# Attention's first loads in another order, its constants made later, and one load of the second layer issued 1.7 slots earlier

## Chip, cores and metric

One core of a Trainium2 chip. The metric is device time in microseconds of one launch, the median of the timed runs. Five engines run side by side: TensorE (PE in the rows, its weight loads PEld), VectorE (DVE), ScalarE (ACT), GpSimd (POOL) and SyncE (SP, which here only issues DMAs). Each runs its own instructions in order and waits on semaphores for the others.

## What is computed

```python
def _attn_ref(q, k, v, phi):           # q, k, v: (8, 8, 576, 64), phi: (8, 8, 576, 32)
    a = np.exp(phi - np.max(phi, axis=2, keepdims=True))
    a = a / (np.sum(a, axis=2, keepdims=True) + 1e-09)
    k_m = np.einsum('bhsm,bhsd->bhmd', a, k)
    v_m = np.einsum('bhsm,bhsd->bhmd', a, v)
    scores = q @ k_m.T / 8;  attn = softmax(scores)
    return attn @ v_m
...
x = attention, as (4608, 512)
x = top-1 mixture of 8 experts of x (w1, w2), times its gate      # moe_
g = elu(x @ w_in);  out = g @ w_out                               # moe2_: 512 -> 2048 -> 512
```

All of it is float32.

## The kernel before

Attention runs over 8 units (`Attn.units`: a pair of batches by half of the heads). What a unit does is cut into steps, methods of `Attn` (L1620 to L1946), and two written lists set the order in which the steps are emitted: `PROLOGUE` for unit 0 and the first pieces of unit 1, then `ORDER` once for each unit, with offsets. A step that stands in `PROLOGUE` is not emitted again by `ORDER`: `attn_items` keeps the first of equal entries. Each engine then runs its instructions in the order in which they were emitted.

The steps that matter here, for unit 0 in their order of need:

- `load_phi`, `load_kv`, `load_q` issue the unit's loads from SP: phi in 2 DMAs of 288 KB into tile `ft`, k and v in 4 of 576 KB into `kv`, q in 2 of 576 KB into `qt`. The tiles have two buffers each, so the loads of unit n+2 wait for the reader of unit n. The hardware DMAs share 8 semaphores in turn, so a DMA also waits until the eighth before it has landed.
- `soft_max` (DVE, the maximum of `ft`), `soft_max_t`, `soft_diag`, `soft_bcast` (PE and DVE, the maximum over all positions), `soft_exp` (DVE subtracts, ACT writes `e`), `soft_sum` (POOL).
- `kvm` (PE, 72 small products of `kv` and `e` into `pkvm`), `kv_sum` (PE), `kv_norm` (DVE, ACT), `kv_t` (PE transposes, ACT writes `kT`, `vT`), `v_gate` (PE with `wgd`, the gate's weights).
- `qtr` (PE transposes q, ACT copies it out as `qT`), `scores` (PE), `scores_exp` and `norm` (DVE, ACT), `attn_t` and `av` (PE, ACT).
- `warm` is products of a tile of ones, only to keep PE busy.

`setup_consts` (L52) runs ahead of all this. It loads the gate's weights `wg` (16 KB), and makes the identity, a triangle `trib`, and tables of numbers: POOL writes each as int32 (`IOTA`), DVE casts it (`iota_f`, L78). All of these but two use one scratch tile `i32`, so that each IOTA waits for the cast before it.

After attention come the experts (TensorE in float32r pieces) and the two layers of the FFN (class `Ffn`), each product by a 7-multiplication scheme, and each operand in two parts, `his` (ACT) and `los` (DVE or POOL). The second layer walks over 36 sets k (9 token tiles by 4 pieces of the hidden dimension). For set k, ACT issues two loads from DRAM tensor `g_d`: `load_g` (768 KB into `los`) and `load_a21` (256 KB into `scr`). Then ACT writes `his` of the three loaded pieces, DVE makes four sums out of `los` and `scr` (`left_sums`, L846 to L849), ACT writes `his` of those, and DVE writes `los` twice (L1271). Only then can PE run the set's 7 products (`prod_out`, L1332 to L1334 for both layers). Sets alternate between two halves of `his` and `los`. The weights `wu` of the last piece (7 DMAs of 512 KB from `woc_d`, L1220) are issued from SP during sets 1 and 2.

The order in the FFN is that of a heap of events with times in slots (a slot is one product); `out_set` puts set k's events at `base(k) = 252 + 7k + 2`, and emits the loads of set k+2 there:

```python
        if 0 < k < NU * NJ - 2:
            ev(b + 3.2, self.load_g, k + 2)
            ev(b + 3.3, lambda: self.load_a21(k + 2, self.scr[k % 2][:, 2]))
        if k and k + 1 < NU * NJ:
            ev(b, self.prep_g, k + 1, b, ev)
```

`prep_g(k+1)` has its events at b (sums), b+0.1 (`his` of the loaded pieces), b+2.0 (`his` of the sums) and later.

Of the kernel before, what the change touches and what calls it, by code (L numbers as in the profile page):

```python
# [37 lines left out]
NT36 = N // P  # L38
# [12 lines left out]

def setup_consts(ctx, tmp_ctx, tc, g, w_gate):  # L52
    nc = tc.nc
    g.cp = ctx.enter_context(tc.tile_pool(name="cp", bufs=1))
    cp = g.cp
    g.ident = cp.tile([P, P], F32, name="ident")
    make_identity(nc, g.ident)
    g.ones = cp.tile([P, P], F32, name="ones")
    nc.vector.memset(g.ones, 1.0)
    g.onesb = cp.tile([P, P], BF16, name="onesb")  # L60
    nc.vector.memset(g.onesb, 1.0)
    g.trib = cp.tile([P, P], BF16, name="trib")
    nc.gpsimd.affine_select(
        out=g.trib, in_=g.onesb, pattern=[[1, P]], compare_op=ALU.is_gt,
        fill=0.0, base=0, channel_multiplier=-1,
    )
    g.wg = cp.tile([P, H // 2, E], F32, name="wg")
    nc.sync.dma_start(g.wg, w_gate.rearrange("(hp r) e -> r hp e", r=P))
    g.wgd = cp.tile([P, H // 2, 2, E], F32, name="wgd")
    nc.gpsimd.memset(g.wgd, 0.0)  # L70
    for h in range(2):
        nc.gpsimd.tensor_copy(g.wgd[64 * h : 64 * h + 64, :, h, :], g.wg[64 * h : 64 * h + 64])
    g.sel = cp.tile([P, 64], F32, name="sel")
    nc.vector.tensor_tensor(out=g.sel, in0=g.ident[:, :64], in1=g.ident[:, 64:], op=ALU.add)
    tmp = tmp_ctx.enter_context(tc.tile_pool(name="ctmp", bufs=1))
    i32 = tmp.tile([P, 128], I32, name="i32")

    def iota_f(name, shape, pattern, base=0, cm=0, dtype=F32):  # L78
        n = 1
        for s in shape[1:]:  # L80
            n *= s
        t = cp.tile(shape, dtype, name=name)
        iv = i32[:, :n]
        nc.gpsimd.iota(iv, pattern=pattern, base=base, channel_multiplier=cm)
        flat = t
        if len(shape) == 3:
            flat = t.rearrange("p a b -> p (a b)")
        nc.vector.tensor_copy(flat, iv)
        return t

    g.rev8 = iota_f("rev8", [P, E], [[-1, E]], base=E)
    g.i128 = iota_f("i128", [P, P], [[1, P]], dtype=BF16)
    g.i36 = iota_f("i36", [P, NT36], [[1, NT36]])
    g.i36b = iota_f("i36b", [P, NT36], [[1, NT36]], dtype=BF16)
    g.kW = iota_f("kW", [P, N // W], [[W, N // W]])
    g.k96 = iota_f("k96", [P, NEARLY * T // 96], [[96, NEARLY * T // 96]], base=96)
    g.tslot = iota_f("tslot", [P, NWIDE + NXMAX], [[1, NWIDE + NXMAX]])
    nid = tmp.tile([P, NT36], I32, name="nid")
    nc.gpsimd.iota(nid, pattern=[[2 * S, B // 2], [1, 9]], base=0, channel_multiplier=9)
    nhi_i = tmp.tile([P, NT36], I32, name="nhi_i")  # L100
    nlo_i = tmp.tile([P, NT36], I32, name="nlo_i")
    nc.vector.tensor_scalar(out=nhi_i, in0=nid, scalar1=6, scalar2=None, op0=ALU.arith_shift_right)
    nc.vector.tensor_scalar(out=nlo_i, in0=nid, scalar1=63, scalar2=None, op0=ALU.bitwise_and)
    g.nhi = cp.tile([P, NT36], BF16, name="nhi")
    g.nlo = cp.tile([P, NT36], BF16, name="nlo")
    nc.vector.tensor_copy(g.nhi, nhi_i)
    nc.vector.tensor_copy(g.nlo, nlo_i)

    g.dram = ctx.enter_context(tc.tile_pool(name="dram", bufs=1, space=DRAM))
    g.x_d = g.dram.tile([N, XW], F32, name="x_d")  # L110
    g.y_d = g.dram.tile([DM, N + PAD], F32, name="y_d")
    g.ord_d = g.dram.tile([N + PAD], I32, name="ord_d")
    g.wic_d = g.dram.tile([NU, P, 7, 2, 2, CW], F32, name="wic_d")
    g.woc_d = g.dram.tile([NU, P, 7, 2, 2, CW], F32, name="woc_d")
    g.g_d = g.dram.tile([NJ, NU, P, 4, 512], F32, name="g_d")
    padz = tmp.tile([1, PAD], I32, name="padz")
    nc.vector.memset(padz, 0)
    nc.sync.dma_start(g.ord_d[N:].rearrange("(o n) -> o n", o=1), padz)
    g.oh = cp.tile([P, NT36, E], BF16, name="oh")
    g.colx = cp.tile([P, NT36], F32, name="colx")  # L120
    nc.vector.memset(g.colx, float(NEARLY * T))


def one_hot(tc, g, pool, lg, bp):
# [184 lines left out]
class Rest:  # L309
# [357 lines left out]
class Small:  # L667
# [18 lines left out]
    def gate(self):  # L686
        self.xn = self.m.x_gate(self.xg)
# [480 lines left out]
class Ffn:  # L1168
# [322 lines left out]
    def out_set(self, k, ev):  # L1491
        b = self.base(k)
        pe = [(1, 0), (2, 1), (4, 2), (6, 3), (7, 4), (5, 5), (3, 6)]
        if k == 0:
            pe = [(1, 0), (2, 0.5), (7, 4), (4, 5), (6, 6), (5, 7), (3, 10.8)]
        if k == NU * NJ - 1:
            pe = [(1, 0), (6, 1), (7, 2), (5, 3), (4, 4), (2, 5), (3, 6)]
        if k == 1:
            pe = [(1, -1), (2, 0), (4, 1.4), (6, 3), (7, 4), (5, 5), (3, 6)]
        for c, at in pe:  # L1500
            ev(b + at, self.prod_out, k, c)
        if 0 < k < NU * NJ - 2:
            ev(b + 3.2, self.load_g, k + 2)
            ev(b + 3.3, lambda: self.load_a21(k + 2, self.scr[k % 2][:, 2]))
        if k and k + 1 < NU * NJ:
            ev(b, self.prep_g, k + 1, b, ev)
        if k % NU == NU - 1:
            ev(b, self.evacuate, k // NU, b, ev)
# [124 lines left out]
class Attn:  # L1633
# [61 lines left out]
                u.qt[:, 2 * b : 2 * b + 2].rearrange("p q i d -> p q (i d)"), self.rows(self.src[0], u, b)  # L1695
            )

    def load_qkv(self, u):
        self.load_kv(u)
        self.load_q(u)  # L1700

    def new(self, u):
        u.xt = self.xbp.tile([P, 2, 9, WV], F32, tag="xt", name="xt", bufs=3)

# [23 lines left out]
    def gate(self, u):  # L1728
        self.gate_oh(u)
        self.gate_x(u)  # L1730

    def soft_max(self, u):
        mx = self.sp.tile([P, 4, M], F32, tag="mx", name="mx")
        m4 = self.sp.tile([P, 4, 4, M], F32, tag="m4", name="m4", bufs=1)
        op = self.tc.nc.vector.tensor_tensor
        ft = u.ft
        op(out=m4, in0=ft[:, :, 0:4, :], in1=ft[:, :, 4:8, :], op=ALU.max)
        op(out=m4[:, :, 0:2, :], in0=m4[:, :, 0:2, :], in1=m4[:, :, 2:4, :], op=ALU.max)
        op(out=mx, in0=m4[:, :, 0, :], in1=m4[:, :, 1, :], op=ALU.max)
        op(out=mx, in0=mx, in1=ft[:, :, 8, :], op=ALU.max)  # L1740
        u.mx = mx
# [208 lines left out]


PROLOGUE = [
    ("load_q", 0),
    ("warm", 0, 0, 15),
    ("load_phi", 0),
    ("load_kv", 0),
    ("load_phi", 1),
    ("load_q", 1),
    ("load_phi", 2),
    ("warm", 0, 1, 4),  # L1960
    ("soft_max", 0),
    ("soft_max_t", 0),
    ("soft_diag", 0),
    ("soft_bcast", 0),
    ("soft_exp", 0),
    ("qtr", 0, (0, 1)),
    ("kvm", 0, 0),
    ("soft_sum", 0),
    ("qtr", 0, (2,)),
    ("soft_max", 1),  # L1970
    ("load_kv", 1),
    ("warm", 0, 2, 4),
    ("kvm", 0, 1),
    ("kv_sum", 0),
    ("kv_norm", 0),
    ("soft_max_t", 1),
    ("qtr", 0, (3,)),
    ("soft_diag", 1),
    ("warm", 0, 3, 8),
    ("soft_bcast", 1),  # L1980
    ("kv_t", 0),
    ("soft_exp", 1),
    ("qtr", 0, (4,)),
    ("v_gate", 0),
]

# [30 lines left out]
    ("soft_bcast", 2),  # L2017
    ("av", 0, 0),
    ("soft_exp", 2),
    ("load_qkv", 2),  # L2020
    ("store", -1),
    ("qtr", 1, (4,)),
    ("v_gate", 1),
# [165 lines left out]
```

## Time and profile before

| | us |
|---|---|
| median of 3 runs | 1345.62 |
| lowest, highest | 1343.79, 1350.82 |
| the profiled execution | 1349.39 |
| its span in the profile | 1347.7 |
| PE busy in it, share of the span | 1302.4, 97% |

The rows below are of the profiled execution. Its time is 3.8 us over the median of the three; what lies outside the span is 1.7 us. In a row of waits, "A <- B: 2.6, 1, 2.6" reads: A waited for B, 2.6 us in total, once, 2.6 us at the longest. "issue" is a wait for nothing that the profile shows.

### The profile page before, as it was taken

How to read it: one execution, taken by the hardware profiler on the slowest of the kernel's cores; microseconds unless marked ns; L12 is line 12 of the kernel's file. 1: busy time of each engine (PE TensorE's matmuls, PEld its weight loads, DVE VectorE, ACT ScalarE, POOL GpSimd, SP SyncE). 2: the span in 40 equal slices, each digit the busy share in tenths (PEclk: the TensorE clock that was granted, in tenths of full speed). 3: DMA queues.
4: the chain of work that ended last, by engine and by line, in shares of the span. 5: the costliest groups of instructions: out<-in, count | busy, mean ns of one | idle time of the engine just before them, and what ended most of it. 6: DMA issues, size and time to landing. Idle time of an engine off the chain costs nothing.

```text
span 1347.7 us, 28034 instructions
## 1 busy us (share of the span) xinstructions
PE 1302.4 (97%) x10938; PEld 1205.0 (89%) x10938; DVE 1042.2 (77%) x1535; ACT 768.3 (57%) x1205; POOL 540.6 (40%) x513
## 2 busy tenths in 40 slices
PE   7888899999999999999999999999999999999998
PEld 6666589999999999999888888888999999999998
DVE  5656778478999989864888888888878877778774
ACT  3556554466566666745787888888843333333331
POOL 3212234467877787735334443433412110122221
PEclk8889889999999999999999999999999999999999
DMA  8888584369888888879843444445984343343431
GB/s 302 287 272 288 135 219 159 105 188 280 263 276 261 273 277 269 270 240 321 316 136 117 133 142 133 138 144 175 334 320 156 127 146 111 132 143 126 156 126 63
DMA packets 190074, 271.56 MB, mean 202 GB/s; under 512 B 16717, under 2 KB 137137, under 8 KB 189938
## 3 DMA queue, kind: packets, MB, share of 16 engines
q1 hardware_dynamic: 164162, 209.02, 47.6%
q10 hardware_dynamic: 19552, 41.42, 9.8%
q0 software_dynamic: 6224, 19.29, 4.6%
q8 instruction: 87, 1.43, 0.4%
q14 instruction: 49, 0.40, 0.1%
HBM read 173.91 MB, written 95.78 MB: 200 GB/s over the span
## 4 chain that ended last, share of the span: by engine, by line
PE 74%; DVE 2%; issue 1%; DMA 1%; ACT 0%; POOL 0%; POOLq 0%; DVEq 0%; ACTq 0%
PE bd L1320 6%; PE bd L1318 6%; PE bd L1319 6%; PE bd L1334 6%; PE bd L1333 6%; PE bd L1332 6%; PE ph L634 4%; PE ph L635 4%; PE acc L651 4%; PE acc L650 4%; PE ph L636 4%; PE acc L649 4%; PE a L1320 2%; PE a L1318 2%; PE a L1319 2%; PE a L1333 2%
## 5 line engine op out<-in xcount | busy, mean ns | idle before, releaser
L1334 PE MATMUL bd<-wu,los 128*128 128x256 f32 x720 | 203.6, 283 | 2.6 <-DVE los L1271 2.6
L1333 PE MATMUL bd<-wu,his 128*128 128x256 f32 x720 | 203.2, 282 | 0.0
L1332 PE MATMUL bd<-wu,his 128*128 128x256 f32 x720 | 202.4, 281 | 0.0
L1523 POOL DMA_INDIRECT out_dram<-o,order x36 | 54.3, 1509 | 298.0 <-DVE o L1518 262.8
L634 PE MATMUL ph<-xh,w1s 128*128 128x288 f32 x500 | 152.6, 305 | 1.3 <-PEq L746 1.1
L651 PE MATMUL acc<-hh,w2s 128*128 128x288 f32 x512 | 151.1, 295 | 0.0
L650 PE MATMUL acc<-hl,w2s 128*128 128x288 f32 x512 | 151.1, 295 | 0.0
L649 PE MATMUL acc<-hh,w2s 128*128 128x288 f32 x512 | 151.0, 295 | 0.0
L1318 PE MATMUL bd<-his,wu 128*128 128x512 f32 (+1 forms) x400 | 149.0, 373 | 0.0
L1320 PE MATMUL bd<-his,wu 128*128 128x512 f32 (+1 forms) x400 | 148.8, 372 | 0.0
L635 PE MATMUL ph<-xl,w1s 128*128 128x288 f32 x500 | 148.1, 296 | 0.5 <-DVE xl L511 0.5
L1319 PE MATMUL bd<-los,wu 128*128 128x512 f32 (+1 forms) x400 | 148.3, 371 | 0.0
L636 PE MATMUL ph<-xh,w1s 128*128 128x288 f32 x500 | 147.5, 295 | 0.0
L1334 PEld LDWEIGHTS bd<-wu,los 128*128 128x128 f32 x720 | 136.2, 189 | 2.8 <-DVE los L1271 2.8
L1333 PEld LDWEIGHTS bd<-wu,his 128*128 128x128 f32 x720 | 136.5, 190 | 0.0
L1332 PEld LDWEIGHTS bd<-wu,his 128*128 128x128 f32 x720 | 136.3, 189 | 0.0
L1271 POOL TENSOR_TENSOR los<-raws,his 128x512 fp32r<-128x512 f32 x64 | 96.1, 1520 | 86.0 <-ACT his L1268 56.0
L639 ACT ACTIVATE hh<-ph 128x288 fp32r<-128x288 f32 x125 | 51.2, 410 | 137.0 <-PE ph L636 130.9
L1268 ACT CAST his<-los 128x1536 fp32r<-128x1536 f32 (+2 forms) x36 | 51.9, 1444 | 129.1 <-DMA los<-g_d 123.5
L1268 ACT CAST his<-scr 128x2048 fp32r<-128x2048 f32 x34 | 64.9, 1908 | 69.9 <-DVE scr L849 69.9
L649 PEld LDWEIGHTS acc<-hh,w2s 128*128 128x128 f32 x512 | 96.1, 188 | 0.0
L650 PEld LDWEIGHTS acc<-hl,w2s 128*128 128x128 f32 x512 | 96.1, 188 | 0.0
(357 smaller groups left out, 3806.3 us busy)
## 6 DMA issues: line engine op xcount, KB each, us to landing
wst<-in_moe_w_dram SPq DMA_DIRECT2D x72, 512.0 KB
los<-g_d ACTq DMA_DIRECT2D x34, 768.0 KB
g_d<-ex SPq DMA_DIRECT2D x128, 128.0 KB
g_d<-ey SPq DMA_DIRECT2D x64, 256.0 KB
wu<-wic_d SPq DMA_DIRECT2D x28, 512.0 KB
wu<-woc_d SPq DMA_DIRECT2D x28, 512.0 KB
qt<-in_q_dram SPq DMA_DIRECT2D x16, 576.0 KB
kv<-in_k_dram SPq DMA_DIRECT2D x16, 576.0 KB
```

The lines of the kernel that those rows point to most:

```text
L634: nc.tensor.matmul(ph, w1h[:, kc, f], xh[:, kc, :], start=(kc == 0), stop=False)
L635: nc.tensor.matmul(ph, w1h[:, kc, f], xl[:, kc, :], start=False, stop=False)
L636: nc.tensor.matmul(ph, w1l[:, kc, f], xh[:, kc, :], start=False, stop=(kc == 3))
L649: nc.tensor.matmul(py[dc], wh, hh, start=(fc == 0), stop=False)
L650: nc.tensor.matmul(py[dc], wh, hl, start=False, stop=False)
L651: nc.tensor.matmul(py[dc], wl, hh, start=False, stop=(fc == 7))
L1318: nc.tensor.matmul(o, w[:, 0, k, f], xh[k], start=s, stop=False, skip_group_check=True)
L1319: nc.tensor.matmul(o, w[:, 0, k, f], xl[k], start=False, stop=False, skip_group_check=True)
L1320: nc.tensor.matmul(o, w[:, 1, k, f], xh[k], start=False, stop=k == 1, skip_group_check=True)
L1332: nc.tensor.matmul(o, gh[:, j, t], w[:, 0, j], start=first, stop=False, skip_group_check=True)
L1333: nc.tensor.matmul(o, gh[:, j, t], w[:, 1, j], start=False, stop=False, skip_group_check=True)
L1334: nc.tensor.matmul(o, gl[:, j, t], w[:, 0, j], start=False, stop=last, skip_group_check=True)
```

## The change

1. `setup_consts` makes only the identity, the tiles of ones, `sel` and a few fills. `wg`'s load becomes a step (`load_wg`), and the rest, on POOL and DVE, becomes the step `consts`, emitted inside the prologue; each table has its own int32 tile.
2. The prologue has another order: phi of unit 0 is loaded first, then its k and v, then q, then unit 1's phi, `wg`, q, k and v. `load_phi` of unit 2 comes after `load_kv` of unit 1. `load_kv` and `load_q` of unit 2 and `load_phi` of unit 3 move from `ORDER` into the prologue. The transposes of q follow `kv_norm`. 8 `warm` products fewer.
3. In the second layer, set 3's loads (k = 1) are emitted 1.7 slots earlier.

```diff
 def setup_consts(ctx, tmp_ctx, tc, g, w_gate):
...
-    nc.gpsimd.affine_select(
-        out=g.trib, in_=g.onesb, pattern=[[1, P]], compare_op=ALU.is_gt,
-        fill=0.0, base=0, channel_multiplier=-1,
-    )
-    nc.sync.dma_start(g.wg, w_gate.rearrange("(hp r) e -> r hp e", r=P))
-    nc.gpsimd.memset(g.wgd, 0.0)
...
-        nc.gpsimd.iota(iv, pattern=pattern, base=base, channel_multiplier=cm)
...
-        nc.vector.tensor_copy(flat, iv)
...
+def late_consts(tc, g, pool):
+    nc = tc.nc
+    nc.gpsimd.affine_select(
+        out=g.trib, in_=g.onesb, pattern=[[1, P]], compare_op=ALU.is_gt,
+        fill=0.0, base=0, channel_multiplier=-1,
+    )
+    counts = []
+    for name, t, base, step in g.iotas:
+        iv = pool.tile(list(t.shape), I32, name=name + "_i", bufs=1)
+        nc.gpsimd.iota(iv, pattern=[[step, t.shape[1]]], base=base, channel_multiplier=0)
+        counts.append((t, iv))
+    nid = pool.tile([P, NT36], I32, name="nid", bufs=1)
+    nc.gpsimd.iota(nid, pattern=[[2 * S, B // 2], [1, 9]], base=0, channel_multiplier=9)
+    for t, iv in counts:
+        nc.vector.tensor_copy(t, iv)
+    nc.vector.tensor_copy(g.i36b, g.i36)
+    for t, op, number in ((g.nhi, ALU.arith_shift_right, 6), (g.nlo, ALU.bitwise_and, 63)):
+        part = pool.tile([P, NT36], I32, tag="nid_p", name="nid_p", bufs=2)
+        nc.vector.tensor_scalar(out=part, in0=nid, scalar1=number, scalar2=None, op0=op)
+        nc.vector.tensor_copy(t, part)
...
         if 0 < k < NU * NJ - 2:
-            ev(b + 3.2, self.load_g, k + 2)
-            ev(b + 3.3, lambda: self.load_a21(k + 2, self.scr[k % 2][:, 2]))
+            ahead = 1.7 if k == 1 else 0
+            ev(b + 3.2 - ahead, self.load_g, k + 2)
+            ev(b + 3.3 - ahead, lambda: self.load_a21(k + 2, self.scr[k % 2][:, 2]))
...
+    def consts(self, u):
+        nc, g = self.tc.nc, self.g
+        nc.gpsimd.memset(g.wgd, 0.0)
+        for h in range(2):
+            nc.gpsimd.tensor_copy(g.wgd[64 * h : 64 * h + 64, :, h, :], g.wg[64 * h : 64 * h + 64])
+        late_consts(self.tc, g, self.sp)
...
 PROLOGUE = [
+    ("load_phi", 0),
+    ("warm", 0, 0, 15),
+    ("load_kv", 0),
     ("load_q", 0),
-    ("warm", 0, 0, 15),
-    ("load_phi", 0),
-    ("load_kv", 0),
...
```

The order of emission as built, in three places. First SP's loads at the start. Before (`ft` is phi, `qt` is q, the pairs go to the two batches of a unit):

```order
L68 DMA wg<-in_moe_w_gate_dram 128x4x8
L1694 DMA qt<-in_q_dram 128x2x576
L118 DMA ord_d<-padz 1x576
L1694 DMA qt<-in_q_dram 128x2x576
L1679 DMA ft<-in_phi_dram 128x2x288 x2
L1687 DMA kv<-in_k_dram 128x2x576
...
L1679 DMA ft<-in_phi_dram 128x2x288 x2
L1694 DMA qt<-in_q_dram 128x2x576 x2
L1679 DMA ft<-in_phi_dram 128x2x288 x2
L1687 DMA kv<-in_k_dram 128x2x576
```

and in the changed kernel:

```order
L1679 DMA ft<-in_phi_dram 128x2x288 x2
L94 DMA ord_d<-padz 1x576
L1687 DMA kv<-in_k_dram 128x2x576
...
L1694 DMA qt<-in_q_dram 128x2x576 x2
L1679 DMA ft<-in_phi_dram 128x2x288 x2
L1730 DMA wg<-in_moe_w_gate_dram 128x4x8
L1694 DMA qt<-in_q_dram 128x2x576 x2
L1687 DMA kv<-in_k_dram 128x2x576
...
L1679 DMA ft<-in_phi_dram 128x2x288 x2
L1687 DMA kv<-in_k_dram 128x2x576
```

Phi of unit 0 went ahead of its q, and the third pair of `ft` loads (unit 2's phi) went behind the k and v of unit 1.

Second, DVE from unit 1's `soft_max` (`m`, `mx`) to unit 0's first `scores_exp` (`sx`) in the changed kernel. Before, the casts stood ahead of unit 0's `soft_max` and between its four operations:

```order
L1747 TENSOR_TENSOR mx<-mx,ft 128x128
L115 CAST rev_75<-rev_i 128x8
L115 CAST i_76<-i_i 128x128
...
L120 CAST nlo<-nid_p 128x36
L1759 TENSOR_REDUCE mb<-psm 128x2
L1761 COPY mbb<-mb 128x128
L1771 TENSOR_TENSOR ft<-ft,psb 128x1152
L1876 COPY bv<-pg 128x2x8
L1744 TENSOR_TENSOR m_448<-ft 128x512
L1745 TENSOR_TENSOR m_448<-m_448 128x4x64
L1746 TENSOR_TENSOR mx<-m_448 128x128
L1747 TENSOR_TENSOR mx<-mx,ft 128x128
L1903 TENSOR_REDUCE sx<-sc 128x16
```

The eleven small operations of the tables now stand ahead of unit 1's `soft_diag` (`mb`). That unit 2's `soft_max` (`m_448`) stands ahead of unit 0's `scores_exp` is as before.

Third, ACT where the second layer's sets 2 and 3 are loaded, before:

```order
L1247 DMA los<-g_d 128x1536
L1251 DMA scr_13084<-g_d 128x512
L1268 CAST his<-los 128x1536
L1268 CAST his<-scr_13084 128x2048
L1247 DMA los<-g_d 128x1536
L1251 DMA scr_13148<-g_d 128x512
L1268 CAST his<-los 128x1536
```

and in the changed kernel:

```order
L1246 DMA los<-g_d 128x1536
L1250 DMA scr_13078<-g_d 128x512
L1267 CAST his<-los 128x1536
L1246 DMA los<-g_d 128x1536
L1250 DMA scr_13142<-g_d 128x512
L1267 CAST his<-scr_13078 128x2048
L1267 CAST his<-los 128x1536
```

Set 3's two loads went ahead of set 2's second cast. The tile `scr_13142` lies where the first layer's `ex` was, so its load waits until the last store of `ex` to `g_d` has landed. Everything else on the five engines keeps its order.

## Rows read from the trace of the kernel before

**Rows 1.** Waits of PE from 300 us to the end, the longest.
```profile
PE bd L1334 <- DVE los L1271: 2.6, 1, 2.6
```
**Rows 2.** Timeline, the start: start, us, engine, line, operation, tiles, [idle before <- releaser].
```profile
10.03 0.69 DVE L1737 TENSOR_TENSOR m<-ft 128x512 f32<-128x512 f32 x1 [4.82 <-DMA ft<-in_phi_dram]
16.39 2.48 PE L1810 MATMUL pkvm<-kv,e 64*32 64x128 f32 x80
27.27 2.08 PE L1882 MATMUL sc<-kT,qT 128*64 128x64 f32 x64
27.50 0.68 DVE L1737 TENSOR_TENSOR m<-ft 128x512 f32<-128x512 f32 x1
30.80 0.68 DVE L1896 TENSOR_REDUCE sx<-sc 128x16 f32<-128x512 f32 x1
34.65 0.69 DVE L1911 TENSOR_TENSOR scs<-scs,ss 128x512 f32<-128x512 f32 x1
36.38 0.37 PE L1820 MATMUL pkvm<-ones,es 64*128 64x1 f32 x1 [2.48 <-issue]
38.14 1.12 PE L1921 MATMUL pta<-ident,scs 128*128 128x128 f32 x4
```
**Rows 3.** Timeline, second layer, columns as in rows 2.
```profile
988.26 0.33 ACTq L1247 DMA_DIRECT2D los<-g_d  x1
992.66 1.48 ACT L1268 CAST his<-los 128x1536 fp32r<-128x1536 f32 x1 [3.40 <-DMA los<-g_d]
994.00 0.32 SPq L1365 DMA_DIRECT2D g_d<-ex  x1
994.75 4.81 SPq L1220 DMA_DIRECT2D wu<-woc_d  x7
996.58 1.91 ACT L1268 CAST his<-scr 128x2048 fp32r<-128x2048 f32 x1 [2.44 <-DVE scr L849]
996.61 0.33 ACTq L1247 DMA_DIRECT2D los<-g_d  x1
997.03 0.65 ACTq L1251 DMA_DIRECT2D scr<-g_d  x1
998.52 2.29 DVE L1271 TENSOR_TENSOR los<-scr,his 128x2048 fp32r<-128x2048 f32 x1
1004.87 1.48 ACT L1268 CAST his<-los 128x1536 fp32r<-128x1536 f32 x1 [6.38 <-DMA los<-g_d]
1006.90 0.69 DVE L846 TENSOR_TENSOR scr<-scr,los 128x512 f32<-128x512 f32 x1 [6.09 <-DMA scr<-g_d]
1009.62 1.76 DVE L1271 TENSOR_TENSOR los<-los,his 128x1536 fp32r<-128x1536 f32 x1
```
**Rows 4.** Stretches: us, PE, PEld, DVE, ACT, POOL busy (count), PEclk, DMA share, GB/s.
```profile
1000.00:1005.00 5.00, 5.00 (x44) 5.00 (x43) 0.81 (x1) 0.13 (x1) 0.00 (x0) 1.00 1.02 419
1005.00:1010.00 5.00, 3.85 (x33) 3.65 (x31) 2.96 (x5) 1.66 (x2) 0.00 (x0) 1.00 0.74 290
1010.00:1015.00 5.00, 3.56 (x20) 3.56 (x21) 3.82 (x3) 2.39 (x2) 0.00 (x0) 0.75 0.64 210
1015.00:1020.00 5.00, 5.00 (x41) 5.00 (x40) 4.97 (x7) 3.16 (x3) 0.00 (x0) 0.91 0.28 69
```
**Rows 5.** A stretch before the weight loads move, columns as in rows 4.
```profile
994.00:996.00 2.00, 2.00 (x19) 2.00 (x19) 1.97 (x4) 0.15 (x1) 0.00 (x0) 1.00 0.41 150
```
**Rows 6.** Stretches of the start, columns as in rows 4.
```profile
10.00:20.00 10.00, 6.67 (x100) 5.32 (x101) 6.10 (x15) 3.72 (x5) 3.75 (x7) 0.66 1.06 387
26.00:28.00 2.00, 1.50 (x36) 1.30 (x38) 1.02 (x3) 1.97 (x4) 0.29 (x1) 1.00 0.44 156
```
**Rows 7.** Waits of PE from 27 to 160 us, two of them.
```profile
PE px L1934 <- issue: 4.7, 2, 2.4
PE pkvm L1810 <- issue: 3.3, 2, 2.7
```
**Rows 8.** DMA queues from 34 to 36.4 us: queue, packets, MB, share.
```profile
q8 instruction: 1, 0.02, 2.8%
```

More of the change, by code (lines that the diff above doesn't have):

```diff
@@ L53, in setup_consts @@
     nc = tc.nc
+    g.w_gate = w_gate
     g.cp = ctx.enter_context(tc.tile_pool(name="cp", bufs=1))
@@ L62, in setup_consts @@
     g.trib = cp.tile([P, P], BF16, name="trib")
-    nc.gpsimd.affine_select(
-        out=g.trib, in_=g.onesb, pattern=[[1, P]], compare_op=ALU.is_gt,
-        fill=0.0, base=0, channel_multiplier=-1,
-    )
     g.wg = cp.tile([P, H // 2, E], F32, name="wg")
-    nc.sync.dma_start(g.wg, w_gate.rearrange("(hp r) e -> r hp e", r=P))
     g.wgd = cp.tile([P, H // 2, 2, E], F32, name="wgd")
-    nc.gpsimd.memset(g.wgd, 0.0)
-    for h in range(2):
-        nc.gpsimd.tensor_copy(g.wgd[64 * h : 64 * h + 64, :, h, :], g.wg[64 * h : 64 * h + 64])
     g.sel = cp.tile([P, 64], F32, name="sel")
@@ L75, in setup_consts @@
     tmp = tmp_ctx.enter_context(tc.tile_pool(name="ctmp", bufs=1))
[L76 to L81, printed above, removed]
-        t = cp.tile(shape, dtype, name=name)
-        iv = i32[:, :n]
-        nc.gpsimd.iota(iv, pattern=pattern, base=base, channel_multiplier=cm)
-        flat = t
-        if len(shape) == 3:
-            flat = t.rearrange("p a b -> p (a b)")
-        nc.vector.tensor_copy(flat, iv)
[L89 to L103, printed above, removed]
+    g.iotas = []
+    for name, shape, dtype, base, step in (
+        ("rev8", [P, E], F32, E, -1),
+        ("i128", [P, P], BF16, 0, 1),
+        ("i36", [P, NT36], F32, 0, 1),
+        ("kW", [P, N // W], F32, 0, W),
+        ("k96", [P, NEARLY * T // 96], F32, 96, 96),
+        ("tslot", [P, NWIDE + NXMAX], F32, 0, 1),
+    ):
+        t = cp.tile(shape, dtype, name=name)
+        setattr(g, name, t)
+        g.iotas.append((name, t, base, step))
+    g.i36b = cp.tile([P, NT36], BF16, name="i36b")
     g.nhi = cp.tile([P, NT36], BF16, name="nhi")
     g.nlo = cp.tile([P, NT36], BF16, name="nlo")
-    nc.vector.tensor_copy(g.nhi, nhi_i)
-    nc.vector.tensor_copy(g.nlo, nlo_i)
     g.dram = ctx.enter_context(tc.tile_pool(name="dram", bufs=1, space=DRAM))
@@ L1696, in load_q @@
             )
-    def load_qkv(self, u):
-        self.load_kv(u)
-        self.load_q(u)
     def new(self, u):
@@ L1730, in gate, with load_wg @@
         self.gate_x(u)
+    def load_wg(self, u):
+        g = self.g
+        self.tc.nc.sync.dma_start(g.wg, g.w_gate.rearrange("(hp r) e -> r hp e", r=P))
+    def consts(self, u):
[4 more added lines that the diff above has]
+        late_consts(self.tc, g, self.sp)
     def soft_max(self, u):
@@ L1952 @@
 PROLOGUE = [
+    ("load_phi", 0),
+    ("warm", 0, 0, 15),
+    ("load_kv", 0),
     ("load_q", 0),
-    ("warm", 0, 0, 15),
-    ("load_phi", 0),
-    ("load_kv", 0),
     ("load_phi", 1),
+    ("load_wg", 0),
     ("load_q", 1),
-    ("load_phi", 2),
-    ("warm", 0, 1, 4),
+    ("load_kv", 1),
     ("soft_max", 0),
@@ L1965 @@
     ("soft_exp", 0),
-    ("qtr", 0, (0, 1)),
+    ("load_phi", 2),
+    ("warm", 0, 1, 8),
     ("kvm", 0, 0),
     ("soft_sum", 0),
[L1969 to L1972, printed above, removed]
     ("kvm", 0, 1),
@@ L1975 @@
     ("kv_norm", 0),
+    ("qtr", 0, (0, 1)),
+    ("soft_max", 1),
+    ("load_kv", 2),
+    ("qtr", 0, (2,)),
+    ("kv_t", 0),
+    ("consts", 0),
     ("soft_max_t", 1),
+    ("soft_diag", 1),
     ("qtr", 0, (3,)),
-    ("soft_diag", 1),
-    ("warm", 0, 3, 8),
+    ("qtr", 0, (4,)),
     ("soft_bcast", 1),
-    ("kv_t", 0),
     ("soft_exp", 1),
-    ("qtr", 0, (4,)),
+    ("load_q", 2),
+    ("load_phi", 3),
     ("v_gate", 0),
@@ L2019 @@
     ("soft_exp", 2),
-    ("load_qkv", 2),
+    ("load_kv", 2),
+    ("load_q", 2),
     ("store", -1),
```

## The prediction, made before the changed kernel was run

> **What bounds the kernel now.** The page first: PE is busy for 97% of the span, so time can only come from the places where PE stands or runs at a lower clock. Then PE's waits, cut at 300 us. After 300 us one wait has any size, 2.6 us of PE for DVE's `los` [rows 1]. It lies in the second layer at set 3, whose loads the change moves. Before 300 us the picture is another: the first scores of unit 0 start at 27.27 us [rows 2], and from then on units follow each other on PE in the order of the list, so attention is a chain on PE that starts when unit 0 is ready. The reader should see in rows 2 what that start hangs on: the first reader of phi, DVE's `m<-ft`, waited until 10.03 us for a load that stands behind q in SP's queue, and the first `kvm` ran at 16.39.
>
> The sum is made against the profiled execution, 1349.4 us. That is 3.8 us over the median of the runs, 1345.6, to which I carry the difference over. About 0.5% (6.7 us) is what a measurement of this kernel can tell from no change.
>
> **The second layer, set 3.** Before, its loads were issued at 996.61 and 997.03, right after set 2's second cast started at 996.58, and that cast had waited for DVE's sums [rows 3]. SP had issued the 7 weight loads from 994.75 on (3.7 MB), so set 3's 768 KB shared the DMA engines with them: its cast started at 1004.87, 8.3 us after the issue, and the sums, which need `scr` too, at 1006.90. From there to the end of `los` at 1009.62 + 1.76 = 1011.38 are 4.5 us, and that ended PE's wait, which had begun 2.6 us before, at about 1008.8.
>
> What the stall costs is read from stretches of 5 us: 44 matmuls undisturbed, then 33, 20 and 41 [rows 4]. 11 + 24 + 3 = 38 missing ones at 5.0 / 44 us are **4.3 us**: 2.6 of standing, the rest at the lower clock that followed, 0.75 and 0.91 on average in the last two stretches.
>
> In the new order set 3's first load is issued behind set 2's first cast, at 992.7. Its only other wait is for PE's products of set 1, which the old order also needed. An undisturbed load of this size took from 988.26 to 992.66, 4.4 us, so it lands at about 997.1; with the old 8.3 us it would be 1001.0. The DMA engines have room just there: 0.41 of their time from 994 to 996 [rows 5]. The second load, 256 KB, now has to wait for the last store of `ex`, issued at 994.00. In the old order it went out 0.42 us after the first, as two issues in a row do, so the store had landed by 997.03, and I take 997.0 for its issue now. From there it has the weight loads beside it. Bounds for its landing: 1001.4 (4.4 us, as the larger undisturbed load) and 1006.9 (as before). I take 1001.9, near the lower end, since the 768 KB that stood ahead of it in ACT's queue are gone; in the old order it came 2.0 us after them. Then set 3's `los` is ready at 1001.9 + 4.5 = 1006.4, 2.4 us before PE asks. Gain **4.3 us**, bounds 0 and 4.3.
>
> Behind that waiting load stand set 2's second cast and the rest of ACT. If the cast starts at 997.0 instead of 996.58, DVE's `los` of set 2 ends at 998.52 + 2.29 + 0.4 = 1001.2. PE needs it at set 2's fourth product of seven. The seven end at about 1008.6, and one is 12 matmuls, 1.36 us, so the fourth starts at 1008.6 - 4 x 1.36 = 1003.2. Two us of cover remain; if the store lands after 999, a stall comes back at set 2.
>
> **The start.** 1.18 MB of q no longer stand ahead of phi and of k and v: 3.0 us at 387 GB/s [rows 6]. The loads also begin about half a microsecond sooner, as `wg` is no longer first. So `kvm` moves from 16.39 to about 12.8. On the way from there to the scores, the transposes and `warm` products that stood between the two parts of `kvm` go behind them or away, and DVE's eleven table operations come in ahead of unit 1's `soft_diag`, gated by POOL's; I let the two cancel at about 1 us each. First scores at 27.3 - 3.6 = **23.7 us**. Bounds: 27.3, if the tables cost 3.6 us on the path, and 22.
>
> **What takes part of it back.** On DVE unit 2's `soft_max` stands ahead of unit 0's `scores_exp`. It started at 27.50 with unit 2's phi long there [rows 2]. Now this phi is loaded behind unit 1's k and v. The bytes up to and with it are those that were under way until the DMA share fell between 26 and 28 us [rows 6], so it lands at 27 to 28 us whatever the scores do. `scores_exp` can then start at about 30.3, against 30.80. Its chain ended at 34.65 + 0.69 = 35.34; `attn_t` (`pta`) came only at 38.14, because PE had stood in a hole of 2.48 us that ended at 36.38. With `norm` over at about 34.9, `attn_t` moves from 38.14 to about 35.0, and the hole, wherever it falls in the meantime, is hidden by this wait. But unit 1's `kv_norm`, behind `norm` on DVE, moves by less, about 1.8 us. Between 3.1 and 1.8 I take **2.5 us** for unit 1's scores and all that follows. Bounds: 0, if phi comes at 28.5 and the hole is not covered, and 5, if 3.6 us and part of the hole come through.
>
> **At no cost.** The removed `warm` products lie where PE waits for loads. The loads of k, v and q of unit 2 and phi of unit 3 go out sooner by part of a unit; their readers are a unit away.
>
> **Sum.** 4.3 + 2.5 = 6.8 us: 1342.6 against the profiled execution, and 1345.6 - 6.8 = **1338.8** as a median.
>
> **The holes.** PE's idle times between 27 and 160 us that nothing in the profile explains are the 2.5 us before 36.38 [rows 2], 4.7 us in two and 3.3 us in two [rows 7]. In the window of the first, the queue for instructions moved one packet beside a full load queue [rows 8]. I read the holes as PE waiting for its next instructions behind the loads; that is an inference. [...]
>
> **Rivals.**
>
> 1. *Only the second layer gains.* The start's 3.6 us are used up by unit 2's late phi. For it: DVE's order. Against: the hole before 36.38 leaves slack. 1345.6 - 4.3 = 1341.3. Chance 0.22.
> 2. *The early load is not early.* `scr` waits for the store, or stays behind the weight loads until 1008.8 - 4.5 = 1004.3 or later, and the stall stays. For it: the wait on the store is new in that place. Against: 150 GB/s where the first load would move [rows 5]. 1345.6 - 2.5 = 1343.1. Chance 0.10.
> 3. *More than forecast.* All of the 3.6 us come through, or a hole falls away: 2.5 us of standing and some 1.7 at the lower clock, as at set 3. 1345.6 - 4.3 - 3.6 = 1337.7 at the least, 1333.5 with a hole less. Chance 0.25.
> 4. *Slower: more holes.* The loads follow each other with fewer gaps. [...] Each new one costs 2.5 + 1.7 = 4.2 us. Two more (8.4) are over the sum: 1345.6 - 6.8 + 8.4 = 1347.2; three make 1351.4, four 1355.6. For it: all five holes lie in attention, where loads run. Against: the loads are a fixed amount, and a gap filled early opens later. Chance 0.05.
>
> **How the numbers follow.** The forecast itself, 1337 to 1341, has 0.38. Faster by over 0.5% means below 1338.9: 0.26 of the forecast's 0.38, as a covered hole adds on that side, and 0.23 of rival 3: 0.49. Slower by over 0.5%, above 1352.3, takes four holes or three and a lost gain: 0.03. The rest, 0.48, is within. The range goes down to 1332.5, rival 3 with a hole less and 1 us for the spread of a median, and up to 1345.0, rival 2 with 2 us for that spread. Left out are rival 4 and the outer parts of rivals 2 and 3, some 0.18.
>
> **What would show it.** In the changed profile: PE's wait for `los` at set 3 gone, its clock 1.00 through it; set 3's first load issued within a microsecond of the start of set 2's first cast, set 2's second cast at most a microsecond later than before. At the start: DVE's first `m<-ft` near 6 us, `kvm` near 12.8, first scores near 23.7, and DVE waiting for phi at unit 2's `soft_max` until 27 to 28. Wrong would be the stall still there at set 3, first scores after 25.5, or attention's later steps moved by something other than 1 to 5 us.

## The result, and the profile after

| | us |
|---|---|
| median of the changed kernel, 6 runs | 1357.14 (1354.91 to 1359.50) |
| median of the kernel before beside it, 6 runs | 1347.02 (1343.79 to 1350.82) |
| ratio, 95% interval | 1.0075, 1.0057 to 1.0092 |
| the profiled execution | 1354.91, span 1353.2 |

The forecast was 1338.8 us, a gain of 6.8. The change costs about 10 us, 7.7 to 12.4 by the interval. The two profiled executions differ by only 5.5 us of span: that of before lies over its median, that of after under its own.

To see where the time goes, DVE's instructions of the two traces were matched, and their starts compared at the same place in the program. The changed kernel is ahead by 1.6 us at 44 us of the old trace, ahead by 2.3 at 64, behind by 0.8 at 76, ahead by 0.6 at 160, behind by 1.5 at 178, by 4.7 at 205, by 7.1 at 350, and by 5.5 at the end. So the new start does arrive sooner. What follows eats it: in attention (from 2.3 ahead at 64 us to 1.5 behind at 178), and twice inside the expert stage, where the prediction's sum has nothing (3.2 us between 186 and 205, 2.0 us between 289 and 295). In the second layer, 1.6 us come back.

The start first, timeline of the changed kernel, columns as in [rows 2], to be read against those rows:

```profile
4.61 0.69 DVE L1744 TENSOR_TENSOR m<-ft 128x512 f32<-128x512 f32 x1 [2.37 <-DMA ft<-in_phi_dram]
12.84 3.06 PE L1817 MATMUL pkvm<-kv,e 64*32 64x128 f32 x136 [0.96 <-DMA kv<-in_v_dram]
21.68 1.97 PE L1801 MATMUL ptq<-ident,qt 128*128 128x128 f32 x8 [1.52 <-DVE mb L1759]
24.61 3.43 PE L1889 MATMUL sc<-kT,qT 128*64 128x64 f32 x64
28.56 1.00 DVE L1744 TENSOR_TENSOR m<-ft 128x512 f32<-128x512 f32 x1 [2.82 <-DMA ft<-in_phi_dram]
30.86 0.68 DVE L1903 TENSOR_REDUCE sx<-sc 128x16 f32<-128x512 f32 x1
34.72 0.69 DVE L1918 TENSOR_TENSOR scs<-scs,ss 128x512 f32<-128x512 f32 x1
37.06 0.33 PE L1889 MATMUL sc<-kT,qT 128*64 128x64 f32 x2 [2.38 <-issue]
37.31 0.66 PE L1928 MATMUL pta<-ident,scs 128*128 128x128 f32 x4
```

`kvm` starts at 11.46 with 8 of its products and, after a wait for v, runs on at 12.84 (forecast 12.8 for its start). The first scores start at 24.61 (forecast 23.7; PE waited 1.5 us for `mb`, which stands behind the tables on DVE). But the scores take 3.43 us in place of 2.08, and unit 2's phi lets DVE's `m` start only at 28.56 (forecast: it lands at 27 to 28), so `scores_exp` starts at 30.86, where it was before. `norm` is over at 34.72 + 0.69 = 35.41, but `attn_t` (`pta`) comes only at 37.31, against 38.14 before, since a hole of 2.38 us stands just ahead of it.

Second, DVE at the expert stage's running sums, timeline of the changed kernel:

```profile
190.46 0.46 DVE L639 SCALAR_TENSOR_TENSOR hl<-ph,hh 128x288 fp32r<-128x288 f32 x1 [2.31 <-ACT hh L638]
195.66 0.75 DVE L168 TENSOR_TENSOR_SCAN scr<-ones,ptot 128x288 f32<-128x288 f32 x1 [4.74 <-DMA x_d<-xt]
196.45 0.45 DVE L171 TENSOR_TENSOR scr<-scr,ptot 128x288 f32<-128x288 f32 x1
```

Before, the second of these rows followed the first with no wait:

```profile
189.35 0.74 DVE L169 TENSOR_TENSOR_SCAN scr<-ones,ptot 128x288 f32<-128x288 f32 x1
```

DVE waits 4.74 us for stores of `xt`, attention's last output tiles. The scan neither reads nor writes them; its tile `scr` now shares memory with them. PE's waits from 150 to 310 us show what comes of it, and a second wait that the kernel before did not have:

```profile
PE pt L613 <- DVE scr L171: 2.3, 1, 2.3
PE ph L635 <- issue: 1.7, 1, 1.7
```

The addresses of the built programs give the reason for the first. The tables' integer tiles now belong to attention's pool `sp`: 1344 bytes per partition more, and the pools above it move up by as much. The topmost of the three buffers of `xt` went from bytes 80320 to 90112 of a partition to 81664 to 91456. The expert stage's `scr` begins at 90112 in both kernels, since a spacer of fixed size (`APART`) puts it there. So `scr` now lies over the last 1344 bytes of an `xt` tile, and its first writer waits, the 4.74 us above, until the stores of `xt` have landed.

Third, set 3 of the second layer, whose two loads both were moved, not one. ACT and SP in the changed kernel, timeline, against [rows 3]:

```profile
999.89 1.48 ACT L1267 CAST his<-los 128x1536 fp32r<-128x1536 f32 x1 [3.53 <-DMA los<-g_d]
999.95 0.33 ACTq L1246 DMA_DIRECT2D los<-g_d  x1
1007.56 0.33 ACTq L1250 DMA_DIRECT2D scr<-g_d  x1
1008.01 1.91 ACT L1267 CAST his<-scr 128x2048 fp32r<-128x2048 f32 x1 [6.64 <-DMA g_d<-ex]
1009.82 1.46 ACT L1267 CAST his<-los 128x1536 fp32r<-128x1536 f32 x1
...
1001.11 0.32 SPq L1364 DMA_DIRECT2D g_d<-ex  x1
1001.86 7.15 SPq L1219 DMA_DIRECT2D wu<-woc_d  x7
```

The large load went out early, as forecast. The small one waited for the last store of `ex` until 1007.56, 6.4 us after the store was issued, and set 2's cast stood behind it until 1008.01. PE's wait for `los` fell only from 2.6 to 2.0 us, and 1.8 of it now stand at set 2:

```profile
PE bd L1333 <- DVE los L1270: 2.0, 2, 1.8
```

Stretches, columns as in [rows 4]:

```profile
1005.00:1010.00 5.00, 5.00 (x44) 4.83 (x42) 0.57 (x2) 1.99 (x2) 0.00 (x0) 1.00 1.02 405
1010.00:1015.00 5.00, 3.19 (x25) 2.97 (x26) 3.31 (x3) 1.28 (x1) 0.00 (x0) 1.00 0.99 392
1015.00:1020.00 5.00, 4.77 (x41) 4.56 (x40) 4.65 (x5) 1.91 (x1) 0.00 (x0) 1.00 0.48 152
```

19 and 3 matmuls are missing where [rows 4] lack 38.

### The profile page after: what moved, and what is told of

The parts are those of the page before. It is cut to its first block, busy times and chain, and to the rows that moved or that the text cites. A ratio compares the mean times of both kernels' runs of the same rounds, so it can differ in the third digit from the quotient of the medians.

```text
span 1353.2 us, 28004 instructions
## 1 busy us (share of the span) xinstructions
PE 1300.5 (96%) x10922; PEld 1203.8 (89%) x10922; DVE 1039.4 (77%) x1535; ACT 767.4 (57%) x1205; POOL 540.9 (40%) x512
## 4 chain that ended last, share of the span: by engine, by line
PE 74%; DVE 2%; DMA 1%; issue 1%; ACT 0%; POOL 0%; POOLq 0%; DVEq 0%; ACTq 0%
PE bd L1319 6%; PE bd L1317 6%; PE bd L1318 6%; PE bd L1333 6%; PE bd L1332 6%; PE bd L1331 6%; PE ph L633 4%; PE ph L635 4%; PE ph L634 4%; PE acc L650 4%; PE acc L649 4%; PE acc L648 4%; PE a L1319 2%; PE a L1317 2%; PE a L1318 2%; PE a L1332 2%
```

## The experiments

Each kernel was timed against the kernel before on the same chip, in 9 to 12 runs; "+6.9 [4.3, 9.4]" is the ratio less one, with its 95% interval, times 1347.5 us.

**Memory alone** (m1), on the kernel before:

```diff
         self.sp = ctx.enter_context(tc.tile_pool(name="sp", bufs=2))
+        ctx.enter_context(tc.tile_pool(name="pad", bufs=1)).tile([P, 336], F32, name="pad")
```

> The kernel before with one unused tile of 1344 bytes per partition ahead of the pool of xt; no instruction is added, only addresses move. Memory theory: the expert stage's table scr now lies over the end of the last xt, so DVE's scan waits for the stores of xt as in the changed kernel (4.74 us of DVE, 2.3 us of PE, then a lower clock): slower than before by 4 to 6 us. Rival, the losses come from holes in attention behind the loads: no change, within 1 us of before.

Measured: +1.3 [-0.9, 3.6], median 1348.64. The wait is there, in DVE's timeline and among PE's waits:

```profile
193.94 0.75 DVE L169 TENSOR_TENSOR_SCAN scr<-ones,ptot 128x288 f32<-128x288 f32 x1 [3.60 <-DMA x_d<-xt]
```
```profile
PE pt L614 <- DVE scr L172: 1.2, 1, 1.2
```

By the matched instructions it costs 2.2 us between 186 and 205 us (3.2 in the changed kernel). So the trace shows the mechanism, smaller than expected, while the times alone would also allow no loss; it is not the whole of the 10 us.

**Memory mended**, on the changed kernel, with the early load of set 3 (m2) and without (m3):

```diff
-APART = 4400
+APART = 4736
```

> The changed kernel with the spacer below scr 1344 bytes larger, so that scr lies above the last xt as before. Memory theory: DVE's wait before the scan goes, and with it 4 to 6 us: about 1351 to 1353 against 1357.1 of the changed kernel, still slower than before by 4 to 6 in the medians, by what attention and the second layer lose. Rival, holes: no change against the changed kernel, 10 us slower than before.

> As the run before it, and the second layer's loads of set 3 where they were. If the early load gains the 1.6 us that the trace suggests (24 matmuls missing from the two stretches at the stall in place of 38), this is 1 to 3 us slower than the run before it. If the early load is worth nothing or loses, the same or faster. Against the kernel before it shows the new start alone: my prediction said 2.5 us faster; the trace says 0 to 4 us slower.

(m3 has `ahead = 0` too; "the run before it" is m2.) Measured: +3.6 [0.9, 6.2] and +4.7 [2.6, 6.7]; medians 1351.79 and 1353.23. DVE's wait is gone in both, but 4 to 5 us of loss are left. By the medians the early load is worth 1.4 us, which is inside the noise of the two. Both still have PE's unexplained wait in the expert stage:

```profile
PE ph L635 <- issue: 2.7, 1, 2.7
```

(the first of the two). That row led to the next group.

**The early load alone** (m4), part 3 of the change on the kernel before.

> The kernel before with the second layer's part of the change alone. Prediction: 4.3 us faster. Rival, from the changed kernel's trace: the second, smaller load waits for the last store of ex, which stands behind the early load in the DMA queues, and set 2's cast behind it; a stall at set 2 of about 2.7 us takes the place of one of 4.3: 1 to 2 us faster.

Measured: -0.4 [-3.6, 2.7], median 1347.35. Its trace shows the same chain as the changed kernel's:

```profile
994.90 0.33 ACTq L1247 DMA_DIRECT2D los<-g_d  x1
1001.35 0.33 ACTq L1251 DMA_DIRECT2D scr<-g_d  x1
1001.80 1.91 ACT L1268 CAST his<-scr 128x2048 fp32r<-128x2048 f32 x1 [5.47 <-DMA g_d<-ex]
```

**The number of warm products.** PE's idle times that nothing in the profile explains ("issue") were counted by the number of the matmul that follows. In all the profiles of this study, 18 kernels, there are 107 of 0.8 us or more between 20 and 400 us, and 106 of them stand, within two, at 12 numbers: 18 at 475, 17 at 1106, 17 at 1488, 18 at 2121, fewer at 347, 726, 853, 979, 1614, 1740, 1868 and 3730, whatever instruction stands there. These numbers lie about 127 or a multiple of it apart, up to 2121. And each of the 107 ended 1.13 to 1.79 us after a packet of 16 KB on the instruction queue ended (median 1.40); these packets (one of 0.02 MB in the window below; 87 with 1.43 MB in the whole profile of before, 16.4 thousand bytes each) are mostly 6 to 7 us apart in attention.

The built programs say what the numbers are. If PE's instructions are counted in program order, the weight loads and a loop that a branch of PE skips included, the instruction behind each of the 107 waits, the odd one at number 223 and those at 3730 included, has a remainder of 194 to 197 of 256. So the holes stand whole multiples of 256 instructions apart. A packet has, by an estimate from the two profiles, about as many: before, PE has 21876 matmuls and weight loads to the 87 packets, 251 each; in the changed kernel 21844 to 88, 248 each. That the queue serves PE, and that the place of a hole is where a new packet begins, is inferred from these numbers and from the packet that comes in just ahead of each end; it is not shown.

In the changed kernel the wait that ended at 300.97 is one. It stands 11 matmuls behind the branch (`PEq`, at 297.60), and the packet before it ended at 299.66. Timeline, and the instruction queue from 297.9 to 299.7 us:

```profile
297.60 0.37 PE L633 MATMUL ph<-xh,w1s 128*128 128x288 f32 x1 [1.22 <-PEq L745]
300.97 0.40 PE L635 MATMUL ph<-xh,w1s 128*128 128x288 f32 x1 [1.67 <-issue]
```
```profile
q8 instruction: 1, 0.02, 6.0%
```

The change takes 8 warm products away, 16 matmul records, so that every later instruction stands 16 numbers lower against these fixed places. Two kernels test this, the changed one (with the larger spacer) with the products back (m5), and the kernel before with 8 fewer (m6):

```diff
-    ("warm", 0, 0, 15),
+    ("warm", 0, 0, 23),
```
```diff
-    ("warm", 0, 0, 15),
+    ("warm", 0, 0, 7),
```

> The changed kernel with the larger spacer, and with the 8 warm products that the change took away put back in the first group, where PE waits for phi. Position theory: holes stand at fixed counts of PE's instructions (the matmuls number 475, 726, 979, 1106, 1488, 1740, 1868 and 2121 in every profile), and 16 fewer matmul records bared one at number 3730 that lay just ahead of a branch of PE before. With them back the hole of 1.3 to 2.7 us in the expert stage goes (PE's wait on issue at the first layer's ph), and with it 2 to 3 us: about 1349. Rival, the hole comes from the traffic there and not from the position: it stays, and the time is as without the products, 1351.8, or up to 1 us longer.

> The kernel before with 8 of its first 15 warm products left out, 16 matmul records, in a place where PE waits 4 us for the first maximum; nothing else. Position theory: a hole of 1.3 to 2.7 us appears in the expert stage near matmul number 3730, 11 matmuls behind PE's branch, and the time is 1.5 to 3 us over before. Rival: no hole there and no change within 1 us; my prediction had these products at no cost.

Measured: -1.1 [-3.2, 1.1], median 1346.20, and +6.9 [4.3, 9.4], median 1353.91. The wait on "issue" is gone in the first and has come into the second; m6 loses more than twice the 1.5 to 3 us expected of that hole. PE's waits from 185 to 310 us in the second; the second row, PE's wait at its branch, is in all 18 kernels (1.1 to 1.6 us):

```profile
PE ph L635 <- issue: 1.8, 1, 1.8
PE ph L634 <- PEq L746: 1.3, 1, 1.3
```

PE idled 5.0 us (4.0 before) at the place where the products were left out, so they cost nothing there: all of this comes later. Nor does the granted clock at the start explain it. From 10 to 20 us it was 0.54 in m6, but also 0.54 in one kernel that has the products (p1, below; 0.66 in the kernel before), and the first scores start at 26.53 us, against 26.26 to 27.89 in the five kernels with the old start and all products. The number of products is the largest single cause in this study.

**Where it comes** (n4). 8 products are left out at the start and 8 put behind `kv_norm` of unit 7, so that only attention is shifted.

> The kernel before with 8 warm products moved from its start to the last unit's part of attention, behind kv_norm of unit 7, where PE waits 0.9 us twice. From there on every instruction has its old number, so the hole near number 3730 is covered again; up to there the numbers are 16 lower, as in the run with 8 products fewer (1353.9, 6.0 over before). If that hole alone made the 6 us: 1348 to 1349. If the holes in attention also grew by the shift: 1350 to 1352.

Measured: +3.4 [1.3, 5.5], median 1351.69, and no wait at 3730. By these times about half of the loss is the expert stage's hole and what follows it, and the other half lies in attention; the intervals of the two runs leave that split uncertain by some 2 us. In m6's own trace the hole costs 2.1 us between 289 and 295 us. In attention the idle time at number 1740 was at most 0.6 us in the 10 kernels with the old position, and 0, 0.64, 2.57, 1.75, 2.58 and 1.48 us in the six that are 16 lower (the changed kernel, m2, m3, m6, o1 and n4). Sums over all places vary from 8.9 to 17.2 us between single executions, and do not settle the rest.

**The change with the products back, memory left as changed** (n2):

> The changed kernel with the 8 warm products put back, and nothing else. Position theory: 5 to 6 us faster than the changed kernel, so about 1351.5, 3 to 5 us slower than before; what is left is DVE's wait for the stores of xt. If position and memory are not two separate causes (if either alone would mend all), it comes out at 1346.

Measured: +0.1 [-1.9, 2.3], median 1349.49. Of the 10 us nothing is left that these runs can tell; the median lies between the two cases expected (1351.5 and 1346). The memory's part is still in it, and it is about as large as what m5, with both mended, gains.

**Both side effects and nothing of the change** (o1), on the kernel before: 7 warm products in the first group, and the unused tile.

> The kernel before with both side effects of the change and nothing of its purpose: 8 of the first 15 warm products left out, and the unused tile of 1344 bytes that puts scr over the last xt. If the two add, 6.0 + 1.3: 7 to 8 us slower than before. If they reinforce each other, as the changed kernel and its two repairs suggest (10.1 with both, 3.6 and 0.1 with one repaired): 10 to 12 us slower.

Measured: +8.4 [5.9, 10.9], median 1356.97. On the kernel before they add (6.9 + 1.3 = 8.2), and make most of what the changed kernel loses, without any of its purpose. On the changed kernel each repair takes off more: the spacer 6.5 us (10.1 to 3.6), the products 10.0 (to 0.1), both 11.2 (to -1.1). Each of these has an interval of 2 to 3 us either way, so whether the two reinforce each other there is open.

**Shifting the other way**, 8 products more, on the kernel before (o2) and on the version with set 3's loads on SP (o3; that version is n3, below):

> The kernel before with 8 more warm products in the first group, where PE waits 2.3 to 4 us for the first maximum: every later instruction of PE is 16 matmul records further on. If the old position is a favourable one, a hole shows near number 3730, now 21 matmuls ahead of PE's branch, and the time is 2 to 5 us over before. If only missing products cost: within 1 us of before, or up to 1 us more by the products' own time.

> The version with set 3's loads on SP (1344.8) with the same 8 more products. If the position makes the cost, it moves by as much as the run before it does against before, within 2 us; if the cost depends on the other details of a kernel, the two differ by more.

Measured: +1.3 [-1.1, 3.9] and -0.8 [-4.0, 2.4], medians 1349.61 and 1350.56. Against their own counterparts both move alike, by 1.3 and by 2.0 us (o3's -0.8 against n3's -2.8); o3's runs fall into two groups (1340.6 to 1344.9 and 1350.0 to 1353.5), so its figure is a weak one. The hole near 3730 that the first case of o2 names is in neither. In these runs it shows only close behind PE's branch: 16 lower, number 3730 stands 10 or 11 matmuls behind the first one after the branch (3719); in the old position it lies 5 ahead of that one (3735), and 16 higher 21 ahead, and shows nothing in both. In instructions of the built programs, if, as inferred above, a packet begins at that remainder: the branch lands some 13 behind the beginning of a packet in the old position, 45 behind it 16 higher, and 20 ahead of the next packet 16 lower. There PE stands 1.6 us (m6) and 1.7 us (the changed kernel) after it has gone on behind the branch; in the others it has 100 matmuls or more to run before the next packet. That the old position is a favourable one is not shown; that 16 lower is a bad one is.

**The start alone.** Spacer and products mended, unit 2's loads in their old place, first with the early load (m8), then without it (n1). In m8's text the first of the four is m5:

> As the first of these four, with the k, v and q of unit 2 and the phi of unit 3 loaded from the second list again, where they were before. If loading them sooner crowds the DMA queues in units 0 to 2 and lengthens the holes there, this is 1 to 3 us faster than the first of these four. If the loads only move and the holes with them, it is within 1 us of it.

> The new start alone, without its two side effects: the changed kernel with the larger spacer, the 8 warm products back, unit 2's loads where they were, and set 3's loads in their old place. My forecast for the start was 2.5 us faster than before (1345.4 in this job's terms, if before is 1347.9). If the start's gain is used up later in attention: within 1 us of before. If the second layer's part was worth the 1.4 us that two earlier runs differ by, this is 1 to 2 us slower than the same kernel with the early loads, 1346.2.

Measured: -2.3 [-5.0, 0.5] and -0.3 [-2.0, 1.6], medians 1346.22 and 1347.45. Loading unit 2 sooner costs nothing measurable (m5, with it, has 1346.20). The start alone gains nothing that these runs can tell.

**Set 3's loads.** Only the large one early, on the kernel before (m7); then both from SP, the large one ahead of the weights and the small one behind the third of them, on n1 (n3; n1 is the first of the four in its text) and on the kernel before (p1):

```diff
-            ev(b + 3.2, self.load_g, k + 2)
+            ev(b + 3.2 - (1.7 if k == 1 else 0), self.load_g, k + 2)
```
```diff
+            if k == 1:
+                ev(b + 1.7, self.on_sync, lambda: self.load_g(3))
+                ev(b + 1.765, self.on_sync, lambda: self.load_a21(3, self.scr[1][:, 2]))
...
-                    ev(end + 5 + 0.02 * i, self.load_wo, u, c)
+                    ev(end + 10.72 + 0.02 * i, self.load_wo, u, c)
```

> The kernel before with only the larger of set 3's two loads (768 KB into los) issued 1.7 slots earlier; the smaller one, which must wait for the last store of ex, stays behind set 2's second cast. Store theory: no stall at set 2, as nothing on ACT waits for the store ahead of the cast; the smaller load is issued at about 997 to 999 and lands beside the weight loads; the stall at set 3 shrinks or goes: 2 to 4 us faster than before. Rival, the smaller load lands as late as before behind the weight loads (1006.9 in the profile of before), and the time stays within 1 us of before.

> As the first of these four, with set 3's two loads issued from SP: the larger one behind the last store of ex and ahead of all 7 weight loads, the smaller one behind the third of them. Theory: the stall at set 3 comes from the queue order alone (the loads stand behind the weights, or the store behind the load); here neither happens, the larger load lands within 5 us, the smaller within 8, PE's wait for los is gone, and the time is 3 to 4.3 us below the first of these four. Rival, the DMA engines have no room for 4.7 MB there: the weights come late instead, PE waits for wu or los at set 3 as long as before, and the time is that of the first of these four.

> The kernel before with set 3's loads issued from SP, ahead of and among the weight loads, and nothing else. If the stall is worth what the forecast gave it, 4.3 us: 1343 to 1344 where before is 1347.9. If it is worth what the version with the new start gained over its twin, 2.6 us: 1345 to 1346. If that gain came from the combination: no change within 1 us.

Measured: +1.5 [-1.1, 4.2], -2.8 [-4.9, -0.9] and -0.7 [-3.0, 1.5]; medians 1348.92, 1344.83 and 1346.46. With only the large load early the rival came true: the small one was issued at 992.82 and DVE, which needs both, waited until 1000.29, 6.1 us, behind the weights; PE's wait is 2.6 us as before. From SP neither stands in the other's way, and PE's wait for `los` falls to 0.4 us (0.7 in p1); timeline and stretches of n3:

```profile
993.01 0.32 SPq L1369 DMA_DIRECT2D g_d<-ex  x1
993.76 0.75 SPq L1246 DMA_DIRECT2D los<-g_d  x1
994.57 1.71 SPq L1219 DMA_DIRECT2D wu<-woc_d  x3
996.39 0.37 SPq L1250 DMA_DIRECT2D scr<-g_d  x1
996.81 2.19 SPq L1219 DMA_DIRECT2D wu<-woc_d  x4
```
```profile
1000.00:1005.00 5.00, 5.00 (x44) 5.00 (x43) 1.32 (x3) 0.16 (x1) 0.00 (x0) 1.00 1.03 415
1005.00:1010.00 5.00, 4.63 (x39) 4.43 (x38) 4.65 (x5) 1.91 (x1) 0.00 (x0) 1.00 0.99 348
1010.00:1015.00 5.00, 5.00 (x44) 5.00 (x44) 3.07 (x5) 1.96 (x2) 0.00 (x0) 1.00 0.19 74
```

5 matmuls are missing instead of 38. Since attention varies so much, the stretch is best measured by itself, between the same two DVE instructions (985.07 and 1060.69 in the trace of before, 75.6 us apart). It takes 74.5 to 78.6 us, 75.8 on average, in the 8 kernels with the old order; 73.6 to 75.6, 74.5, in the 6 with both loads early from ACT; and 72.9, 73.0 and 73.7 in the three with the loads from SP. By these averages the early load of the change is worth 1.3 us, though the two ranges overlap, and the loads from SP 2.6; their three lie below all others. The whole time does not show it everywhere: n3 is 2.5 us below n1, a little less than the 3 to 4.3 expected, but p1 alone (-0.7) fits its third case, no change, as well as a gain of 2.6.

n3 has the lowest median of the study, and of the 16 intervals its own is the only one wholly below the kernel before; p1 and o3, with the same loads, do not repeat that. It carries the new start without its two side effects, unit 2's loads in their old place, and set 3's loads from SP.

## Why the prediction was wrong

**The step that failed** is the one with the fewest words: "The removed `warm` products lie where PE waits for loads", at no cost. Their time was indeed covered. What they did otherwise was to hold every later instruction of PE at its number, and the holes go by these numbers (106 of 107 at 12 of them). Taking 8 away cost 6.9 us [4.3, 9.4] on the kernel before. I had the direction as rival 4, more holes, at 4.2 us each, with a chance of 0.05: I tied the holes to the load queue alone and counted loads, not instructions. The rows that would have told were there: the holes' matmul numbers in the old trace, 475, 1106, 1488, 1868 and 2121, differ by multiples of about 127 (my list of the holes left out the one at 1868, 1.1 us). These numbers do not reach across the branch, since the skipped loop lies between; the count of instructions in the two built programs does, and it would have shown the remainder of the holes, 194 to 197 of 256, coming up right behind the branch.

The holes were not small either: their sum in attention was 8.9 to 17.2 us in every execution. PE also waits 1.1 to 1.6 us at its branch in every kernel, and the hole at 3730 appears only in the five where that number stands 10 or 11 matmuls behind the first one after the branch. Why the one goes with the other is not shown.

**A second term was missing**, the addresses. That the change leaves the order of the rest alone was not enough: nine small tiles in another pool moved `xt` by 1344 bytes onto the reach of `scr`, and DVE got a wait that no order of instructions shows. It cost 1.3 us [-0.9, 3.6] by the times, 2.2 to 3.2 by the traces.

**The second layer**, a gain of 4.3 us forecast, measured 1.3 in the stretch and 0.4 [3.6 faster, 2.7 slower] alone. The price of the stall was high, but of the right order: the loads from SP take 2.6 us off it and leave 5 matmuls missing, and part of the 38 in [rows 4] was a lower clock, 0.75 in one stretch, that four of the other seven executions with the old order do not show behind their stall. What failed is "I take 997.0": I took the time at which the store of `ex` had landed from the old order, in which the large load was not yet ahead of it. With that load in front the store took 6.4 us (5.4 in m4, 5.5 in m7) and not at most 3.0; in n3, where it goes first, at most 3.4. Rival 2 had the place ("`scr` waits for the store"), and the warning on set 2 ("if the store lands after 999, a stall comes back at set 2") came true as it stood.

**The start**, a gain of 2.5 us forecast, measured 0.3 faster [2.0 faster, 1.6 slower] alone (n1). Its first steps came within 1.4 us: `m` at 4.61 (about 6 forecast), `kvm` at 11.46 and 12.84, first scores at 24.61. What failed is "the hole, wherever it falls in the meantime, is hidden by this wait". It does not move with the work: it stayed at matmul number 475, from 34.68 to 37.06 us, and held `attn_t` 1.9 us beyond the end of `norm`. With unit 2's phi at 28.56, half a microsecond after the end of the range I gave, this is my lower bound as it stands, "0, if phi comes at 28.5 and the hole is not covered". The scores also ran mostly at a lower granted clock (0.55 from 24 to 28 us; 1.00 in the old kernel from 26 to 30), but they ended at 28.04, ahead of phi. In the trace of the changed kernel 1.6 us were left at 44 us and 2.3 at 64; the medians do not show them at the end.

The sum as measured: 6.9 for the position, 1.3 for the memory, and what is left of the two gains, -0.3 and -0.4 alone (-1.1 together in m5, -2.3 in m8), makes 6 to 7.5 against 10.1 [7.7, 12.4]. The three or four microseconds between are within the intervals of the terms, and what they are, chance or two effects that reinforce each other, is open. The half of the position's cost that lies in attention is shown by time only; that it comes from number 1740 and its neighbours is likely by the rows, and not shown.

## What to carry to other kernels

Where a kernel is bound by PE and its loads run close, an edit's side effects can outweigh its purpose, as in o1 (8.4 us of loss with nothing of the purpose): count how many instructions it adds to or takes from the engine that is the bound (8 products, 6.9 us [4.3, 9.4] here), and what it does to the addresses of every pool above the tile it adds (1344 bytes, 1.3 us [-0.9, 3.6] here). Both can be tested alone, by a few idle products and an unused tile on the kernel before, at no risk to what is computed, before the change itself is judged. And a load that is moved forward goes in front of something: ask which store or load that one waits for, and take its landing time from the new queue, not from the old (6.4 us against at most 3.0 for the store here).

## What the runs showed that I had not expected

- PE's holes stand whole multiples of 256 of its instructions apart (a remainder of 194 to 197 in all 107), and each ends 1.13 to 1.79 us after a packet of 16 KB on the instruction queue has come in (107 of 107). Whether one shows, and how long it is, differs between executions: at number 1106 it was 0.67 to 4.18 us.
- Eight warm products, which cost no time where they stand, are worth 6.9 us by their number.
- Single executions differ far more in attention than the medians do: the kernel before, m4, m7 and p1 have the same instructions up to the second layer, and reach the same DVE instruction near the end of attention at 154.9, 156.6, 148.5 and 149.9 us. A forecast of 2 us made from one such trace, as mine for the start, lies inside that spread.
- A 256 KB store issued 1.2 us after a 768 KB load, on another queue, landed 6.4 us after its issue; without that load ahead of it, in at most 3.0 (before) and 3.4 us (n3).
